# Row preparation of six experts from GpSimd to VectorE, in a planned attention and mixture-of-experts kernel

## The chip, the cores and the metric

The kernel runs on one core of a Trainium2 chip. Its engines are TensorE (PE: matmuls, with PEld for the loading of weights), VectorE (DVE), ScalarE (ACT), GpSimd (POOL) and SyncE (SP), each with a queue of its own that it works through in order, and 16 DMA engines that move data between HBM and the on-chip memories SBUF and PSUM. The metric is device microseconds of one execution; the median of several runs counts.

## The reference

```python
# attention without softmax: 8 batches x 8 heads, sequence 576, head size 64
kv  = einsum('bhsd,bhse->bhde', k, v)
out = einsum('bhsd,bhde->bhse', q, kv)
out = out / sqrt(mean(out*out, -1) + 1e-6) * g_norm
x   = out.transpose(0, 2, 1, 3).reshape(4608, 512)
# top-1 mixture of experts: 8 experts, D = 512, F = 1024, capacity 1152
logits = x @ w_gate; e = argmax(logits, 1); gate = softmax(logits)[e]
for each expert e:                      # its tokens in order, up to the capacity
    y = relu(x[tokens] @ w1[e]) @ w2[e]
    out[tokens] = gate * y              # tokens over the capacity: 0
```

All tensors are fp32.

## The kernel before

The first part of the execution (about its first quarter) computes attention and writes the un-normalized rows, with their norm factors and the gate, to `x_dram`: 4608 rows of 8 x (64 + 8) columns. Then the experts are worked through in order of their load, r = 0 to 7, with fixed budgets of 704, 672, 640, 624, 592, 576, 560 and 512 rows, so 6, 6, 5, 5, 5, 5, 5 and 4 tiles of up to 128 rows.

fp32 products are made from f16 halves: a value's high half is its f16 rounding, its low half the f16 rounding of the rest, and a product is high x high + high x low + low x high. Both the weights and the rows of an expert have to be split so.

For an expert beside the products of the one before (`rows_beside`), each tile of rows is gathered by POOL's indirect DMA (`xg`, L438), normalized (`xm` = `xg` x norm factor, `norm`, L446), its gate column copied (`gt`, L453, POOL), its high half cast by ScalarE (`pair_high`, L472), its low half made as `xm` - high (`pair_low`, L476), and the pair transposed into `xs` by a DMA of SP (L481). For the second expert (r = 1) the plan may put `xm` on VectorE or POOL, for the others on POOL alone; `pair_low` is always on POOL. Each POOL operation of the two is followed by an `engine_nop`.

The weights (`weights`, `split_weight`) come in fp32 to `raw` by eight DMAs of SP. VectorE takes the largest absolute value per partition (`am`, L342, eight per matrix; `a`, L350), multiplies that of w1 by the norm's weight `gcol`, one value per partition (L352); TensorE turns it to a row (`pt_max`, L355), VectorE takes the maximum (`bm`, L359), TensorE spreads it to all partitions (L362), VectorE makes a power of two of it (`bmax`, `ew`, `sw`, L366 and L300 to L309) and for w1 multiplies that by `gcol` (`sg`, L371). Then ScalarE makes the high halves `w1h`, `w2h` (L376) and VectorE the low ones `w1l`, `w2l` (L382), eight pieces each.

The products of an expert (`products`): for each of eight j, the first gemm makes a block `hp` in PSUM from 24 matmuls (two column halves each while there are over 512 rows: 16 with `w1h` and the high halves of the rows, then with their low halves; 8 with `w1l`; the trace merges them as x16 and x8). ScalarE makes `hh` = relu(`hp`) in f16 (L535), VectorE the rest `hl` (L538). `hp` has two banks: the product for j + 2 waits for `hl` of j. The second gemm makes `yp` (L576, narrow tiles L585, turned back by VectorE's copy `yt` L591 and TensorE L596), ScalarE scales it by the gate (`ysb`, L601), and POOL scatters it to the output (L606).

What stands in which order is set by one planner (`Plan`). Each operation has ways (engine and planned duration), what it depends on, a key, buffers that it takes from rings (`xg` 4, `xm` 2, `pair` 2, `xs` 2, `h` 2), and `late`, a time added to the earliest start that its dependencies allow. The planner places whatever can start first, the lower key ahead, and the program is issued on each engine in the planned order. At run time an engine holds to that order: an instruction that has to wait keeps all that stand behind it.

Of the kernel before, what the change touches and what calls it, by code (L numbers as in the profile page):

```python
# [15 lines left out]
ALU = mybir.AluOpType  # L16
# [29 lines left out]
FIRST = -50.0  # L46
# [21 lines left out]
NORM = 1.22  # L68
PAIR = 1.33
TURN = 1.25  # L70
TURNED = 1.3
GATHER = 1.2


class Hold:
# [91 lines left out]
def attention_moe_kernel(  # L167
# [12 lines left out]
    nc = tc.nc  # L180
# [4 lines left out]
    P = 128  # L185
# [143 lines left out]
    def split_weight(i, ws, raw, pieces=8):  # L329

        z = {}
# [16 lines left out]
        def most():  # L348
            z["a"] = a1 = sm.tile([P, 1], F32, name=f"a1_{i}")
            nc.vector.tensor_reduce(out=a1, in_=am(), axis=AX.X, op=ALU.max)  # L350
            if i == 0:
                nc.vector.tensor_tensor(out=a1, in0=a1, in1=gcol, op=ALU.mult)  # L352

        def across(pt):
            nc.tensor.transpose(pt[0:1, 0:P], z["a"], ident)  # L355
# [8 lines left out]
        def scale(pb):  # L364
            z["b"] = sm.tile([P, 1], F32, name="bmax")
            nc.vector.tensor_copy(z["b"], pb[:, 0:1])  # L366
            z["e"] = exponent(z["b"], 30, f"ew{i}")
            z["s"] = pow2(z["e"], -1, (256, 268)[i], f"sw{i}")
            if i == 0:
                sg = sm.tile([P, 1], F32, name="sg")  # L370
                nc.vector.tensor_tensor(out=sg, in0=z["s"], in1=gcol, op=ALU.mult)  # L371
                z["s"] = sg

        def high(p, e="A"):
# [45 lines left out]
    class Rows:  # L420
# [50 lines left out]
            self.pair[i] = self.pool.tile([P, 2, DM], F16, name="pair", bufs=2)  # L471
            nc.scalar.copy(self.pair[i][0:n, 0], self.xm[i][0:n])  # L472

        def pair_low(self, i):
            n, pair = self.part(i)[1], self.pair[i]
            nc.gpsimd.tensor_tensor(out=pair[0:n, 1], in0=self.xm[i][0:n], in1=pair[0:n, 0], op=ALU.subtract)  # L476
            nc.gpsimd.engine_nop()

        def pair_turn(self, i):
            x, n, _ = self.part(i)  # L480
# [187 lines left out]
    op = plan.op  # L668
# [857 lines left out]
    def weights(r, key, after, after2):  # L1526

        ws, sets, zs, holds = wsets[r % 2], [], [], []
        for i in range(2):
# [29 lines left out]
                f["across"](x.t[:, 128:256])  # L1559

            o = op(("V", 0.3), lambda e, f=f: f["most"](), tops, FIRST)
            o = op(("T", 0.12), across, [o], FIRST, (x,), late=2.0)
            o = op(("V", 0.2), lambda e, f=f, x=x: f["across_max"](x.t[:, 128:256]), [o], FIRST, (), (x,))
            o = op(("T", 0.06), lambda e, f=f, x=x: f["back"](x.t[:, 0:1]), [o], FIRST, (), (x,), late=1.0)
            ew = new(f"e{i}")
            o = op(("V", 1.1), lambda e, f=f, x=x: f["scale"](x.t[:, 0:1]), [o], FIRST, (ew,), (x,))
            zs.append((z, o, ew))
# [9 lines left out]
    def rows_beside(r, key):  # L1577
# [9 lines left out]
        for i in range(n):  # L1587
            xg, xm, pair = new("xg"), new("xm"), new("pair")

            def fetch(e, i=i):  # L1590
                if i == 0:
                    st["x"] = Rows(mo, st["gi"], 0, BUDGET[r], BM, 4)
                st["x"].fetch(i)

            o = op(("P", 1.05), fetch, [cut_, first] + early.get(("lows", r - 1), [])[-1:], key, (hold, xg), (sl,))
            first = first or o
            asked.append(o)
            o = op(("D", GATHER), None, [o], key, (), (xg,))
            a = op([("V", 0.61), ("P", NORM)] if r == 1 else ("P", NORM),
                   lambda e, i=i: st["x"].norm(i, nc.vector if e == "V" else nc.gpsimd), [o], key - 5 if r == 1 else key + 1,  # L1600
                   (xm,), (xg,))
            gates.append(op(("P", 0.25), lambda e, i=i: st["x"].gate(i, nc.gpsimd), [a], key + 1, (), (xg, hold)))
            a = op(("A", 0.52), lambda e, i=i: st["x"].pair_high(i), [a], key + 1, (pair,), (xm, hold))
            a = op(("P", PAIR), lambda e, i=i: st["x"].pair_low(i), [a], key + 1, (), (xm, pair, hold))
            if r == 1:
                early.setdefault(("lows", r), []).append(a)
            a = op(("S", TURN), lambda e, i=i: st["x"].pair_turn(i), [a], key + 1, (), (pair, hold))
            sent.append(a)
            turned.append(op(("D", TURNED), None, [a], key + 1, (), (pair, hold)))
# [107 lines left out]
```

## Time and profile before

| | us |
|---|---|
| median of three timed runs | 569.93 (567.73 to 570.16) |
| profiled execution | 566.6 |
| its span | 564.8 |
| TensorE busy | 520.2 (92%) |
| VectorE busy | 382.5 (68%) |
| ScalarE busy | 252.7 (45%) |
| GpSimd busy | 207.1 (37%) |

The busy share of an engine is an average over the attention part and the experts, which have other limits; it is read stretch by stretch below. A wait is put down to the operation whose end released it. The mean granted clock of TensorE in the profiled execution is 0.981 of full speed.

### The profile page before, as it was taken

How to read it: one execution, taken by the hardware profiler on the slowest of the kernel's cores; microseconds unless marked ns; L12 is line 12 of the kernel's file. 1: busy time of each engine (PE TensorE's matmuls, PEld its weight loads, DVE VectorE, ACT ScalarE, POOL GpSimd, SP SyncE). 2: the span in 40 equal slices, each digit the busy share in tenths (PEclk: the TensorE clock that was granted, in tenths of full speed). 3: DMA queues.
4: the chain of work that ended last, by engine and by line, in shares of the span. 5: the costliest groups of instructions: out<-in, count | busy, mean ns of one | idle time of the engine just before them, and what ended most of it. 6: DMA issues, size and time to landing. Idle time of an engine off the chain costs nothing.

```text
span 564.8 us, 12345 instructions
## 1 busy us (share of the span) xinstructions
PE 520.2 (92%) x4727; PEld 343.2 (61%) x4727; DVE 382.5 (68%) x978; ACT 252.7 (45%) x508; POOL 207.1 (37%) x233
## 2 busy tenths in 40 slices
PE   4989897978979997998999999999999999999995
PEld 4878786855536564544664575487467648745442
DVE  4468899899949979999997286367729606721200
ACT  1748684876313661644633526252544525202210
POOL 3011013552255684755225640644373171012011
PEclk9979996999999998999999999999999999999999
DMA  8999999592277687795938562664666151001001
GB/s 278 376 354 301 384 390 373 176 317 96 96 232 254 144 302 166 201 306 132 277 109 236 112 224 66 169 171 161 167 140 214 39 114 39 1 38 40 0 30 40
DMA packets 78020, 102.60 MB, mean 182 GB/s; under 512 B 43222, under 2 KB 51414, under 8 KB 76932
## 3 DMA queue, kind: packets, MB, share of 16 engines
q1 hardware_dynamic: 69600, 70.43, 42.5%
q0 software_dynamic: 7776, 31.30, 15.6%
q8 instruction: 39, 0.64, 0.5%
q14 instruction: 25, 0.20, 0.1%
q10 hardware_dynamic: 580, 0.02, 0.1%
HBM read 73.13 MB, written 20.61 MB: 166 GB/s over the span
## 4 chain that ended last, share of the span: by engine, by line
PE 26%; issue 16%; DMA 5%; DVE 3%; POOL 1%; ACT 1%; POOLq 0%; DVEq 0%; ACTq 0%
PE yp L576 12%; PE hp L530 12%; DMA out_dram<-ysb,si 5%; DVE w2l L382 1%; PE yp L585 1%; POOL xg L438 1%; DVE hl L538 1%; ACT w1h L376 0%; ACT w2h L376 0%; POOL xm L446 0%; POOLq L1652 0%; POOL pair L476 0%; POOL out_dram L606 0%; PE pt_max L355 0%; PE pt_max L362 0%
## 5 line engine op out<-in xcount | busy, mean ns | idle before, releaser
L530 PE MATMUL hp<-xs,w1h 128*128 128x320 f16 (+6 forms) x896 | 134.4, 301 | 5.1 <-DVE hl L538 4.5
L530 PEld LDWEIGHTS <-w1h 128*128 128x128 f16 x960 | 93.4, 98 | 47.1 <-issue 8.8
L576 PEld LDWEIGHTS <-hh 128*128 128x128 f16 x560 | 54.4, 98 | 65.5 <-issue 2.9
L606 POOL DMA_INDIRECT out_dram<-ysb,si x41 | 42.8, 1043 | 137.3 <-ACT ysb L601 99.6
L535 ACT ACTIVATE hh<-hp 128x320 f16<-128x320 f32 (+7 forms) x64 | 40.8, 638 | 114.5 <-PE hp L530 111.9
L342 DVE TENSOR_REDUCE am<-raw 128x1 f32<-128x512 f32 x120 | 75.6, 673 | 4.1 <-DMA raw<-in_moe_w_dram 3.8
L530 PE MATMUL hp<-xs,w1l 128*128 128x320 f16 (+6 forms) x448 | 72.0, 301 | 0.0
L538 DVE SCALAR_TENSOR_TENSOR hl<-hp,hh 128x320 f16<-128x320 f32 (+7 forms) x64 | 47.2, 737 | 32.9 <-ACT hh L535 32.8
L476 POOL TENSOR_TENSOR pair<-xm,pair 128x512 f16<-128x512 f32 (+5 forms) x35 | 44.7, 1278 | 66.5 <-ACT pair L472 61.8
L576 PE MATMUL yp<-w2h,hh 128*128 128x512 f16 x272 | 64.4, 379 | 0.8 <-ACT ysb L601 0.8
L576 PE MATMUL yp<-w2l,hh 128*128 128x512 f16 x272 | 64.6, 379 | 0.0
L576 PE MATMUL yp<-w2h,hl 128*128 128x512 f16 x272 | 64.3, 379 | 0.0
L601 ACT ACTIVATE ysb<-yp,ysc 128x512 f32<-128x512 f32 (+5 forms) x40 | 27.3, 684 | 82.4 <-PE yp L576 73.1
L382 DVE SCALAR_TENSOR_TENSOR w2l<-raw,sw,w2h 128x512 f16<-128x512 f32 x64 | 53.8, 885 | 10.7 <-ACT w2h L376 9.9
L530 PEld LDWEIGHTS <-w1l 128*128 128x128 f16 x480 | 46.9, 98 | 19.5
L438 POOL DMA_INDIRECT xg<-x_dram,gi x41 | 42.3, 1031 | 40.1 <-DVE gi L640 27.0
L382 DVE SCALAR_TENSOR_TENSOR w1l<-raw,sg,w1h 128x512 f16<-128x512 f32 x64 | 47.5, 797 | 0.9 <-ACT w1h L376 0.8
L576 PEld LDWEIGHTS <-hl 128*128 128x128 f16 x280 | 27.0, 98 | 31.9
L823 PE MATMUL op<-kv_bd,qt 128*128 128x144 f32 x256 | 42.6, 310 | 3.7 <-ACT qt L676 1.3
L376 ACT ACTIVATE w2h<-raw,sw 128x512 f16<-128x512 f32 x62 | 39.8, 711 | 5.2 <-DVE p2t L307 2.1
L376 ACT ACTIVATE w1h<-raw,sg 128x512 f16<-128x512 f32 x60 | 38.3, 711 | 7.2 <-DVE sg L371 7.1
L823 PEld LDWEIGHTS op<-kv_bd,qt 128*128 128x128 f32 x256 | 36.7, 206 | 6.0 <-ACT qt L676 2.2
(246 smaller groups left out, 688.7 us busy)
## 6 DMA issues: line engine op xcount, KB each, us to landing
raw<-in_moe_w_dram SPq DMA_DIRECT2D x64, 512.0 KB
k_sb<-in_k_dram SPq DMA_DIRECT2D x16, 576.0 KB
v_sb<-in_v_dram SPq DMA_DIRECT2D x16, 576.0 KB
x_dram<-o_sb POOLq DMA_DIRECT2D x8, 1152.0 KB
q_sb<-in_q_dram SPq DMA_DIRECT2D x16, 512.0 KB
x_dram<-o_sb POOLq DMA_DIRECT2D x8, 144.0 KB
q_sb<-in_q_dram SPq DMA_DIRECT2D x32, 32.0 KB
xg<-x_dram,gi POOLq DMA_INDIRECT x41
```

Source lines behind the costliest of these rows:

```text
L342: nc.vector.tensor_reduce(out=am()[:, p:p + 1], in_=raw[:, sl(p)], axis=AX.X, op=ALU.max, apply_absolute_value=True)
L376: nc.scalar.activation(wh[:, sl(p)], raw[:, sl(p)], AF.Copy, scale=z["s"])
L382: nc.vector.scalar_tensor_tensor(out=wl[:, sl(p)], in0=raw[:, sl(p)], scalar=z["s"], in1=wh[:, sl(p)], op0=ALU.mult, op1=ALU.subtract)
L438: nc.gpsimd.indirect_dma_start(out=self.xg[i][0:n], out_offset=None, in_=x_dram[0:self.rows, :], in_offset=bass.IndirectOffsetOnAxis(ap=se ...
L476: nc.gpsimd.tensor_tensor(out=pair[0:n, 1], in0=self.xm[i][0:n], in1=pair[0:n, 0], op=ALU.subtract)
L530: nc.tensor.matmul(self.view(hp)[:, u], lhsT=w[:, c, j * P:(j + 1) * P], rhs=x[:, c, u * hw:(u + 1) * hw], start=(t == 0 and c == 0), stop ...
L535: nc.scalar.activation(self.out(self.hh, j), self.view(hp), AF.Relu)
L538: nc.vector.scalar_tensor_tensor(out=self.out(self.hl, j), in0=self.view(hp), scalar=0.0, in1=self.out(self.hh, j), op0=ALU.max, op1=ALU.s ...
L576: nc.tensor.matmul(yp[0:n, 0:DM], lhsT=h[:, j, o:o + n], rhs=w[:, j, :], start=(m == 0), stop=(m == len(self.terms) - 1))
L601: nc.scalar.activation(self.ysb[0:n], yp[0:n, 0:DM], AF.Copy, scale=self.ysc[0:n, i:i + 1])
L606: nc.gpsimd.indirect_dma_start(out=out[:, :], out_offset=bass.IndirectOffsetOnAxis(ap=self.sidx[0:n, col:col + 1], axis=0), in_=ysb[0:n], ...
L823: nc.tensor.matmul(y, lhsT=qt.t[:, i * P:(i + 1) * P], rhs=kv2[:, half * HH + i], start=True, stop=True)
```

## The change

From the third expert on (r = 2 to 7), `norm` and `pair_low` are operations of VectorE (planned 0.64 us each) and no longer of POOL (1.22 and 1.33); `norm` is planned at least 3.0 us (`LANDED`) later than before after its gather. The gate's copy stays on POOL, and so do both operations for r = 1. The two products with `gcol` become `tensor_scalar` with `gcol` as the scalar operand. In the plan, `across` (the transpose of the maximum) is late by 5.0 in place of 2.0, `back` by 3.0 in place of 1.0. Lines behind L72 move down by 1, those behind `pair_low` by 2.

```diff
--- before.py
+++ after.py
@@ -70,6 +70,7 @@
 TURN = 1.25
 TURNED = 1.3
 GATHER = 1.2
+LANDED = 3.0
 
 
 class Hold:
@@ -349,7 +350,7 @@
             z["a"] = a1 = sm.tile([P, 1], F32, name=f"a1_{i}")
             nc.vector.tensor_reduce(out=a1, in_=am(), axis=AX.X, op=ALU.max)
             if i == 0:
-                nc.vector.tensor_tensor(out=a1, in0=a1, in1=gcol, op=ALU.mult)
+                nc.vector.tensor_scalar(out=a1, in0=a1, scalar1=gcol, scalar2=None, op0=ALU.mult)
 
         def across(pt):
             nc.tensor.transpose(pt[0:1, 0:P], z["a"], ident)
@@ -368,7 +369,7 @@
             z["s"] = pow2(z["e"], -1, (256, 268)[i], f"sw{i}")
             if i == 0:
                 sg = sm.tile([P, 1], F32, name="sg")
-                nc.vector.tensor_tensor(out=sg, in0=z["s"], in1=gcol, op=ALU.mult)
+                nc.vector.tensor_scalar(out=sg, in0=z["s"], scalar1=gcol, scalar2=None, op0=ALU.mult)
                 z["s"] = sg
 
         def high(p, e="A"):
@@ -471,10 +472,11 @@
             self.pair[i] = self.pool.tile([P, 2, DM], F16, name="pair", bufs=2)
             nc.scalar.copy(self.pair[i][0:n, 0], self.xm[i][0:n])
 
-        def pair_low(self, i):
+        def pair_low(self, i, eng=nc.gpsimd):
             n, pair = self.part(i)[1], self.pair[i]
-            nc.gpsimd.tensor_tensor(out=pair[0:n, 1], in0=self.xm[i][0:n], in1=pair[0:n, 0], op=ALU.subtract)
-            nc.gpsimd.engine_nop()
+            eng.tensor_tensor(out=pair[0:n, 1], in0=self.xm[i][0:n], in1=pair[0:n, 0], op=ALU.subtract)
+            if eng is nc.gpsimd:
+                nc.gpsimd.engine_nop()
 
         def pair_turn(self, i):
             x, n, _ = self.part(i)
@@ -1559,9 +1561,9 @@
                 f["across"](x.t[:, 128:256])
 
             o = op(("V", 0.3), lambda e, f=f: f["most"](), tops, FIRST)
-            o = op(("T", 0.12), across, [o], FIRST, (x,), late=2.0)
+            o = op(("T", 0.12), across, [o], FIRST, (x,), late=5.0)
             o = op(("V", 0.2), lambda e, f=f, x=x: f["across_max"](x.t[:, 128:256]), [o], FIRST, (), (x,))
-            o = op(("T", 0.06), lambda e, f=f, x=x: f["back"](x.t[:, 0:1]), [o], FIRST, (), (x,), late=1.0)
+            o = op(("T", 0.06), lambda e, f=f, x=x: f["back"](x.t[:, 0:1]), [o], FIRST, (), (x,), late=3.0)
             ew = new(f"e{i}")
             o = op(("V", 1.1), lambda e, f=f, x=x: f["scale"](x.t[:, 0:1]), [o], FIRST, (ew,), (x,))
             zs.append((z, o, ew))
@@ -1596,12 +1598,14 @@
             first = first or o
             asked.append(o)
             o = op(("D", GATHER), None, [o], key, (), (xg,))
-            a = op([("V", 0.61), ("P", NORM)] if r == 1 else ("P", NORM),
-                   lambda e, i=i: st["x"].norm(i, nc.vector if e == "V" else nc.gpsimd), [o], key - 5 if r == 1 else key + 1,
-                   (xm,), (xg,))
+            by_letter = {"V": nc.vector, "P": nc.gpsimd}
+            a = op([("V", 0.61), ("P", NORM)] if r == 1 else ("V", 0.64),
+                   lambda e, i=i: st["x"].norm(i, by_letter[e]), [o], key - 5 if r == 1 else key + 1,
+                   (xm,), (xg,), late=0.0 if r == 1 else LANDED)
             gates.append(op(("P", 0.25), lambda e, i=i: st["x"].gate(i, nc.gpsimd), [a], key + 1, (), (xg, hold)))
             a = op(("A", 0.52), lambda e, i=i: st["x"].pair_high(i), [a], key + 1, (pair,), (xm, hold))
-            a = op(("P", PAIR), lambda e, i=i: st["x"].pair_low(i), [a], key + 1, (), (xm, pair, hold))
+            a = op(("P", PAIR) if r == 1 else ("V", 0.64), lambda e, i=i: st["x"].pair_low(i, by_letter[e]), [a], key + 1, (),
+                   (xm, pair, hold))
             if r == 1:
                 early.setdefault(("lows", r), []).append(a)
             a = op(("S", TURN), lambda e, i=i: st["x"].pair_turn(i), [a], key + 1, (), (pair, hold))
```

Two places show how the order moves. First VectorE in the second expert's first gemm, where `hl` is this expert's and `am`, `a` are maxima of the third expert's weights. Before:

```order
L382 SCALAR_TENSOR_TENSOR w2l_2715<-raw_2711,sw_3342,w2h_2714 128x512 x2
L538 SCALAR_TENSOR_TENSOR hl<-hp,hh 128x672
L382 SCALAR_TENSOR_TENSOR w2l_2715<-raw_2711,sw_3342,w2h_2714 128x512 x2
L342 TENSOR_REDUCE am_3492<-raw_151 128x1
L538 SCALAR_TENSOR_TENSOR hl<-hp,hh 128x672
L342 TENSOR_REDUCE am_3492<-raw_151 128x1 x5
L538 SCALAR_TENSOR_TENSOR hl<-hp,hh 128x672
L342 TENSOR_REDUCE am_3492<-raw_151 128x1 x2
L342 TENSOR_REDUCE am_3555<-raw_2711 128x1
L350 TENSOR_REDUCE a_0_3567<-am_3492 128x1
L352 TENSOR_TENSOR a_0_3567<-a_0_3567,gcol 128x1
```

Two `w2l`, then maxima, stand between one `hl` and the next here. With the change, from the second of these `hl` on; `xm` and `pair` are the third expert's rows:

```order
L540 SCALAR_TENSOR_TENSOR hl<-hp,hh 128x672
L383 SCALAR_TENSOR_TENSOR w2l_2715<-raw_2711,sw_3365,w2h_2714 128x512 x3
L540 SCALAR_TENSOR_TENSOR hl<-hp,hh 128x672
L383 SCALAR_TENSOR_TENSOR w2l_2715<-raw_2711,sw_3365,w2h_2714 128x512 x2
L447 TENSOR_TENSOR xm<-xg 128x512 x2
L540 SCALAR_TENSOR_TENSOR hl<-hp,hh 128x672
L477 TENSOR_TENSOR pair<-xm,pair 128x512 x2
L343 TENSOR_REDUCE am_3347<-raw_151 128x1 x2
L540 SCALAR_TENSOR_TENSOR hl<-hp,hh 128x672
L343 TENSOR_REDUCE am_3347<-raw_151 128x1
L447 TENSOR_TENSOR xm<-xg 128x512 x2
L343 TENSOR_REDUCE am_3347<-raw_151 128x1
```

The `w2l` of the second expert stand ahead of what they stood behind, and between two `hl` there are now up to five operations, `xm` and `pair` among them.

POOL at the same place, before: `xg` are gathers of the third expert's rows, ISA is the `engine_nop`.

```order
L438 DMA xg<-x_dram,gi_2817 128x576
L446 TENSOR_TENSOR xm<-xg 128x512
L449 ISA
L476 TENSOR_TENSOR pair<-xm,pair 128x512
L477 ISA
L453 COPY gt<-xg 128x1
L476 TENSOR_TENSOR pair<-xm,pair 128x512
L477 ISA
L446 TENSOR_TENSOR xm<-xg 128x512
```

Tile by tile, gathers alternate here with `xm`, `pair` and `gt`. With the change:

```order
L439 DMA xg<-x_dram,gi_2817 128x576
L454 COPY gt<-xg 128x1
L439 DMA xg<-x_dram,gi_2817 128x576
L454 COPY gt<-xg 128x1 x4
L439 DMA xg<-x_dram,gi_2849 128x576 x4
L608 DMA out_dram<-ysb,si_2789 4608x512
L454 COPY gt<-xg 128x1
```

Gathers and gate copies follow one another, and those of the fourth expert (another `gi`) come right behind.

## Rows read from the trace of the kernel before

**Rows 1.** Part 1 of the page: busy us, share of the span, instructions

```profile
PE 520.2 (92%) x4727; PEld 343.2 (61%) x4727; DVE 382.5 (68%) x978; ACT 252.7 (45%) x508; POOL 207.1 (37%) x233
```

**Rows 2.** Stretches; columns: us, then per engine busy (instructions), PEclk, DMA share, GB/s

```profile
200.00:260.00 60.00, 54.22 (x309) 30.42 (x310) 56.42 (x98) 28.30 (x46) 37.29 (x41) 0.97 0.79 238
260.00:300.00 40.00, 38.55 (x339) 25.86 (x337) 38.21 (x78) 22.86 (x37) 13.19 (x15) 1.00 0.63 183
300.00:500.00 200.00, 199.55 (x1494) 128.33 (x1493) 118.68 (x280) 78.58 (x127) 79.90 (x90) 1.00 0.48 128
```

**Rows 3.** What TensorE waited for, 195 to 565: us in total, times, longest

```profile
PE hp L530 <- DVE hl L538: 4.5, 3, 3.7
PE pt_max L362 <- DVE bm L359: 2.2, 2, 1.2
PE yp L596 <- DVE yt L591: 0.7, 1, 0.7
PE hp L530 <- DMA xs<-pair: 0.5, 1, 0.5
PE pt_max L355 <- DVE a L352: 0.5, 1, 0.5
```

**Rows 4.** Timeline of TensorE: start us, us, engine, line, operation [idle before <-releaser]

```profile
207.14 2.44 PE L530 MATMUL hp<-xs,w1h 128*128 128x336 f16 x16
...
210.56 2.44 PE L530 MATMUL hp<-xs,w1h 128*128 128x336 f16 x16
...
217.85 3.73 PE L530 MATMUL hp<-xs,w1h 128*128 128x336 f16 x16 [3.70 <-DVE hl L538]
...
222.94 2.44 PE L530 MATMUL hp<-xs,w1h 128*128 128x336 f16 x16
...
265.74 2.34 PE L530 MATMUL hp<-xs,w1h 128*128 128x320 f16 x16
```

**Rows 5.** Timeline of VectorE, same columns

```profile
209.04 0.86 DVE L538 SCALAR_TENSOR_TENSOR hl<-hp,hh 128x672 f16<-128x672 f32 x1 [0.25 <-ACT hh L535]
209.82 6.62 DVE L382 SCALAR_TENSOR_TENSOR w2l<-raw,sw,w2h 128x512 f16<-128x512 f32 x2
...
216.96 0.84 DVE L538 SCALAR_TENSOR_TENSOR hl<-hp,hh 128x672 f16<-128x672 f32 x1
...
240.21 6.60 DVE L382 SCALAR_TENSOR_TENSOR w2l<-raw,sw,w2h 128x512 f16<-128x512 f32 x8
...
252.26 2.88 DVE L352 TENSOR_TENSOR a<-a,gcol 128x1 f32<-128x1 f32 x1
...
260.53 2.66 DVE L371 TENSOR_TENSOR sg<-sw,gcol 128x1 f32<-128x1 f32 x1
```

**Rows 6.** Lines L382 and L446 on VectorE: ns min/median/max, first and last start, forms

```profile
L382 DVE SCALAR_TENSOR_TENSOR w2l<-raw,sw,w2h x64: 715/741/5954, 141.3 to 477.7; 128x512 f16<-128x512 f32 x64
...
L446 DVE TENSOR_TENSOR xm<-xg x7: 681/693/1735, 161.6 to 193.1; 128x512 f32<-128x512 f32 x5, 64x512 f32<-64x512 f32 x1, 32x512 f32<-32x512 f32 x1
```

**Rows 7.** Timeline of GpSimd

```profile
209.69 1.07 POOL L446 TENSOR_TENSOR xm<-xg 128x512 f32<-128x512 f32 x1
...
215.19 1.28 POOL L453 COPY gt<-xg 128x1 f32<-128x1 f32 x2
...
250.74 2.30 POOL L476 TENSOR_TENSOR pair<-xm,pair 128x512 f16<-128x512 f32 x2
253.02 2.09 POOL L446 TENSOR_TENSOR xm<-xg 128x512 f32<-128x512 f32 x2
...
259.83 2.29 POOL L476 TENSOR_TENSOR pair<-xm,pair 128x512 f16<-128x512 f32 x2
```

**Rows 8.** Part 5 of the page: busy us, mean ns of one, idle before, releaser

```profile
L342 DVE TENSOR_REDUCE am<-raw 128x1 f32<-128x512 f32 x120 | 75.6, 673 | 4.1 <-DMA raw<-in_moe_w_dram 3.8
```

**Rows 9.** The waits of all engines

```profile
POOL pair L476 <- ACT pair L472: 61.8, 10, 13.3
```

**Rows 10.** Timeline of VectorE, earlier

```profile
167.94 0.68 DVE L446 TENSOR_TENSOR xm<-xg 64x512 f32<-64x512 f32 x1 [2.21 <-DMA xg<-x_dram,gi]
```

## The prediction

> **What bounds the kernel now.** I read the busy shares first, then a table of stretches, then what TensorE waited for, then the timelines of the three engines around the longest wait. TensorE is busy for 520.2 of 564.8 us [rows 1], and from 300 to 500 for 199.55 of 200 [rows 2]: whatever is saved ahead of that stretch moves its dense work up and shortens the span by as much, and nothing can be gained inside it. What is left lies in 200 to 300, where 5.8 and 1.45 us of TensorE are idle [rows 2]. The waits from 195 on sum to 8.4 us [rows 3]: 4.5 for `hl`, 2.2 for `bm`, 0.5 for `a` (all three made by VectorE, DVE), 0.7 for `yt` and 0.5 for a transpose's DMA.
>
> The longest of them is the key. In the second expert's first gemm a group of products starts every 3.42 us (207.14, 210.56); the next one is due at 213.98, but starts at 217.85 after 3.70 us without work [rows 4]. It waits for `hl` at 216.96, and that stood on DVE behind two `w2l` that began at 209.82 and took 6.62 us [rows 5], where two cost 1.48 at the median of 741 ns and one took 5954 ns [rows 6]. In that time GpSimd (POOL) worked on `xm`, `pair` and `gt` from 209.69 to 216.47 [rows 7], and `w2l` ended when POOL did. After the wait TensorE is slow for one group: 5.09 us to the start of the next (222.94), not 3.42 [rows 4], 1.67 us more. [...]
>
> The same pattern stands twice more: `a` x `gcol` (one element per partition) takes 2.88 us at 252.26, beside POOL's `pair` and `xm` from 250.74 to 255.11, and `sg` = `sw` x `gcol` takes 2.66 us at 260.53, beside a `pair` run that begins at 259.83 [rows 5, 7]. So in this trace a DVE instruction with two operands in SBUF stands still while POOL runs back to back on tiles in SBUF, to the end of POOL's run and not of one instruction.
>
> [...]
>
> **The change part by part.** The third to eighth expert have 5, 5, 5, 5, 5 and 4 tiles of rows, 29 in all; for each, one `xm` and one `pair` leave POOL for DVE.
>
> 1. The hold in the second expert's gemm. The POOL run beside it belongs to the third expert's rows, so it goes; in the new order POOL has there only gathers and one-column copies. `w2l` then costs its median, `hl` comes on time, and the 3.70 us and the 1.67 us behind it go: 5.37 us. Late next in that group would be `hl` behind the new `xm` and `pair`, which step 5 counts.
>
> 2. The two tiny products. Their waits on TensorE are 0.5 for `a` and 2.2 for `bm` (two of them, one behind each of the held products) [rows 3]: 2.7 us. They go twice over: POOL's run is gone, and the product reads `gcol` as a scalar, not as a second tensor. Between nothing and 2.7 I take 2.7.
>
> 3. The other two waits for `hl`, 4.5 - 3.7 = 0.8 us [rows 3], also stand behind `w1l` and `w2l` of a slot that the new order fills otherwise. 0 to 0.8; I take 0.8, as long POOL runs are gone there too.
>
> 4. Margins. The transposes of the maxima (`pt_max`) are planned 3 and 2 us later after what they need. Their real waits are under 1.2 us [rows 3], so TensorE meets them ready. What comes later is the scale and with it `w1h`, `w1l`, `w2h`, `w2l` of the next expert. For the third expert that has room: its first gemm starts at 265.74 [rows 4], some 9 us earlier after the gain, and its `w2l` is done at 246.81 [rows 5], 10 us ahead of that. The second expert has none: its `w2l` is still being made inside its own first gemm, at 209.82 [rows 5]. There 0.7 for `yt` and 0.5 for the DMA can go [rows 3], or up to 5 us of planned lateness appear. I take +0.5, with -3 to +1.2 as the ends.
>
> 5. What it costs on DVE. 58 instructions at the nearest row, `xm` on DVE, of which seven are there with 681, 693 and 1735 ns [rows 6]: 40 us at the median, 39 to 101 at the ends. `pair` on DVE is not in the trace; it has the same shape and also two SBUF operands, so it gets the same row. I take 40. That lies beside TensorE: DVE is busy 118.68 of 200 us from 300 to 500 [rows 2], and 10 instructions per expert are 7 us in some 50. From 200 to 300 it is busy 94.63 of 100, but that includes the holds, 5.2 us of it in the one `w2l` (5.954 - 0.741). With the 5.4 that DVE is idle there, 10.6 us of room against 7 of new work an expert.
>
> What counts there is `hl`. One that came on time ran from 209.04 to 209.90, 0.66 us before the group that needs its bank (210.56) [rows 4, 5], and took 0.86. Per 3.42 us DVE has 3.42 - 0.86 = 2.56 for other work. By the new order the work between `hl`s is two `w2l` and two `xm` (2.9 us), two `pair` and two `am` (2.7), then two `am`, two `xm` and a `pair` (3.4), with `am` at 673 ns [rows 8]. Over 2.56 each that is 0.3, 0.2 and 0.9, summed 1.4 us late, against 0.66 that is free: about 0.7 us of wait. Ends: 0, and a stall of 5.4 each time (the second rival). I take -0.7.
>
> 6. What POOL loses, 29 `xm` and 29 `pair`, shortens nothing: it is busy 37% [rows 1]. Gathers and scatters may start earlier. The gathers wait for free `xg` slots, which DVE now frees; the ring has four. 0.
>
> The sum is 5.37 + 2.7 + 0.8 + 0.5 - 0.7 = 8.7 us. The profiled run took 566.6 us, 1.8 of it outside its span; it would take 557.9. It is 3.3 us below the median of the three timed runs, 569.93 (567.73 to 570.16). As the terms are waits of the order and not of one run, I take them off the median: **561.2 us**.
>
> **The rivals.**
>
> A smaller gain. The wider margins push the second expert's scales back, and its first product waits for `w1h` or `w1l` at about 200. Up to 5 us are planned, some of it is covered by the 1.2 us that TensorE waits there already: about 3 us less, 569.9 - 6 = 564. For it: the second expert's scales have no time in hand (step 4). Against: the second expert's last `pair`, which is what TensorE waits for last, comes earlier in the new order.
>
> Slower: DVE takes over POOL's waits. POOL's `pair` waited for ScalarE's cast 61.8 us in 10 places, up to 13.3 [rows 9], and a DVE `xm` waited 2.21 us for its gather [rows 10]. POOL can stand there at no cost. On DVE everything behind it stands too, `hl` first, and `hl` has 0.66 us. A wait like that hold costs what the hold costs, 3.70 + 1.67 = 5.4 us. One such stall in three of the six experts, 16.2, against 8.7 is +7.5: 577. It decides from a second stall on (8.7 / 5.4 = 1.6). For it: the 61.8. Against: ScalarE's cast waited on POOL's `xm` itself, DVE's is faster, and the order puts other DVE work between an `xm` and its `pair` (`hl` or `am`), and leaves 3 us after a landing.
>
> The hold is not POOL's. If 5.954 us for one `w2l` came from elsewhere, the stalls stay, and DVE has 10 more instructions, 6.9 us, in a stretch that is full: 569.9 + 6.9, again about 577. [...] Against: two holds end where POOL's runs end (216.44 and 216.47, 255.14 and 255.11), and the third begins inside one [rows 5, 7].
>
> No gain. The stalls go but the next work waits for something as late: the third expert's rows or weights, needed 9 us earlier: 569.9. For it: no row gives the landing of the third expert's transposes in the new order. Against: the weights have 10 us in hand (step 4), and DMA is at 0.79 of its time in this stretch only, 0.63 and 0.48 behind it [rows 2].
>
> **How the numbers follow.** The forecast (558 to 563.5): 0.50. Smaller gain: 0.22. No gain: 0.10. DVE's waits: 0.11. Another cause of the hold: 0.03. More gain, to below 556: 0.04. A measurement of this kernel, with timed runs 0.43% apart, can tell about 0.5% from no change, 2.8 us. Faster: 0.50 + 0.22 + 0.04 = 0.76; the same: 0.10; slower: 0.14. From 556 to 571 only the last case and the two slow ones are left out, 0.18.
>
> **What would show it.** Right: no DVE `w2l` above 2 us from 200 on, groups of the second expert's first gemm 3.42 us apart throughout, `bm` and `a` gone from TensorE's waits, the third expert's products starting at about 257, DVE up by some 30 us in its busy time (40 less the holds). Wrong: `hp` waiting for `hl` again with DVE's own wait for ScalarE's `pair` or a gather ahead of it; TensorE waiting for `w1h` or `w1l` near 200; or `w2l` held though POOL only moves rows.

## The result and the profile after

| | us |
|---|---|
| median with the change, 20 runs | 563.57 (559.96 to 568.55) |
| median before, 20 runs | 569.71 (565.47 to 574.35) |
| ratio, 95% interval | 0.9892 [0.9869, 0.9915] |
| profiled execution, span | 562.91, 561.1 |

The change makes the kernel 6.1 us faster (1 - 0.9892 of 569.71; 4.8 to 7.5 by the interval). 561.2 was forecast, 8.7 us below the first median of 569.93: the direction holds, the time lies within the range, and the gain is 2.6 us short.

Busy time of the profile after (part 1 of the page). VectorE is up 20 us on [rows 1], not the 30 that were forecast; GpSimd loses 58.

```profile
PE 518.4 (92%) x4727; PEld 342.6 (61%) x4727; DVE 402.6 (72%) x1037; ACT 253.3 (45%) x508; POOL 148.8 (27%) x174
```

The three stretches (us, busy time and instructions of PE, PEld, DVE, ACT, POOL, PEclk, DMA share, GB/s), against [rows 2]: TensorE now has 1.46 and 0.56 us idle in the first two, not 5.8 and 1.45, and 0.96 from 300 to 500, where it had 0.45. The granted clock is 1.00 in the first, where it was 0.97. Before, it was 0.50 of full speed from 218.9 to 222.2, in the slow group of products behind the long wait; half of these 3.3 us is 1.7 us, about the 1.67 that this group took more. That is gone too.

```profile
200.00:260.00 60.00, 58.54 (x466) 34.89 (x463) 52.38 (x103) 29.52 (x48) 23.91 (x25) 1.00 0.83 239
260.00:300.00 40.00, 39.44 (x285) 25.12 (x281) 33.29 (x72) 19.74 (x31) 9.87 (x11) 1.00 0.62 169
300.00:500.00 200.00, 199.04 (x1494) 127.89 (x1492) 150.92 (x346) 83.50 (x133) 42.69 (x53) 1.00 0.51 134
```

What TensorE waited for from 195 on (us in total, times, longest), against [rows 3]: `bm`, `a` and the DMA are gone, `yt` doubled, and `hl` still costs 1.1 us in two other places.

```profile
PE yp L598 <- DVE yt L593: 1.5, 1, 1.5
PE hp L532 <- DVE hl L540: 1.1, 2, 0.6
PE hp L532 <- DVE p2t L308: 0.3, 1, 0.3
```

TensorE's timeline at the second expert, against [rows 4]: behind the wait for `yt` the second group follows after 3.63 us (a product with `bm` lies between), the others every 3.42 us, and the third expert starts at 260.63, 56.5 us after the second, where it was 66.1 (199.60 to 265.74).

```profile
203.68 0.60 PE L598 MATMUL yp<-ident,yt 128*64 128x128 f32 x4 [1.46 <-DVE yt L593]
204.11 2.44 PE L532 MATMUL hp<-xs,w1h 128*128 128x336 f16 x16
...
207.74 2.44 PE L532 MATMUL hp<-xs,w1h 128*128 128x336 f16 x16
...
211.16 2.44 PE L532 MATMUL hp<-xs,w1h 128*128 128x336 f16 x16
...
214.58 2.44 PE L532 MATMUL hp<-xs,w1h 128*128 128x336 f16 x16
...
260.63 1.65 PE L532 MATMUL hp<-xs,w1h 128*128 128x320 f16 x11
```

VectorE's two lines of the low halves (ns min/median/max), against [rows 6]: no `w2l` is held any more (751 ns at most); one `w1l` still takes 2202.

```profile
L383 DVE SCALAR_TENSOR_TENSOR w1l<-raw,sg,w1h x64: 729/735/2202, 108.1 to 450.4; 128x512 f16<-128x512 f32 x64
L383 DVE SCALAR_TENSOR_TENSOR w2l<-raw,sw,w2h x64: 706/743/751, 145.4 to 473.8; 128x512 f16<-128x512 f32 x64
```

That one is in the eight `w1l` of the second expert, whose rows are still GpSimd's; `yt` stands behind them, and TensorE for `yt`:

```profile
195.26 7.74 DVE L383 SCALAR_TENSOR_TENSOR w1l<-raw,sg,w1h 128x512 f16<-128x512 f32 x8
...
203.13 0.40 DVE L593 COPY yt<-yp 128x256 f32<-128x256 f32 x1
```

The wait for `p2t` and the longer one for `hl` (0.32 and 0.64 us) begin in the fourth expert's gemm: VectorE stands 5.25 us on the copy of an index table (`si`), which waits for a scatter that still reads the buffer, and `hl` stands behind.

```profile
319.85 0.17 DVE L642 COPY si<-sidx_tab 128x6 int32 x1 [5.25 <-DMA out_dram<-ysb,si]
...
320.99 0.80 DVE L540 SCALAR_TENSOR_TENSOR hl<-hp,hh 128x624 f16<-128x624 f32 x1
```

The shorter wait for `hl`, 0.49 us in the third expert's gemm (at 271.73), has another cause. VectorE waited 1.90 us for ScalarE's cast, and from then on the work ahead of that `hl` is late:

```profile
264.80 0.69 DVE L477 TENSOR_TENSOR pair<-xm,pair 128x512 f16<-128x512 f32 x1 [1.90 <-ACT pair L473]
```

VectorE's own waits of these two kinds, 200 to 500. ScalarE's cast is what the slower rival named; here it is 10.3 us in 11 places:

```profile
DVE pair L477 <- ACT pair L473: 10.3, 11, 3.6
...
DVE si L642 <- DMA out_dram<-ysb,si: 5.7, 2, 5.2
```

### The profile page after: what moved, and what is told of

Read it like the earlier page. It is cut to its first block, busy times and chain, and to the rows that moved or that the text cites. A ratio compares the mean times of both kernels' runs of the same rounds, so it can differ in the third digit from the quotient of the medians.

```text
span 561.1 us, 12271 instructions
## 1 busy us (share of the span) xinstructions
PE 518.4 (92%) x4727; PEld 342.6 (61%) x4727; DVE 402.6 (72%) x1037; ACT 253.3 (45%) x508; POOL 148.8 (27%) x174
## 4 chain that ended last, share of the span: by engine, by line
PE 44%; issue 18%; DVE 17%; DMA 16%; ACT 2%; POOL 1%; POOLq 0%; SPq 0%; DVEq 0%; ACTq 0%
PE hp L532 18%; PE yp L578 13%; DMA out_dram<-ysb,si 10%; PE op L825 4%; DVE w1l L383 3%; DMA q_sb<-in_q_dram 2%; DVE ss L858 2%; PE qp L807 2%; PE a L736 1%; PE yp L587 1%; DVE am L343 1%; DVE hl L540 1%; DMA xg<-x_dram,gi 1%; DMA v_sb<-in_v_dram 1%; DMA xs<-pair 1%
## 5 line engine op out<-in xcount | busy, mean ns | idle before, releaser
L608 POOL DMA_INDIRECT out_dram<-ysb,si x41 | 47.2, 1150 | 243.9 <-ACT ysb L603 197.6
L439 POOL DMA_INDIRECT xg<-x_dram,gi x41 | 40.5, 988 | 43.0 <-DVE xm L447 10.4
L383 DVE SCALAR_TENSOR_TENSOR w2l<-raw,sw,w2h 128x512 f16<-128x512 f32 x64 | 44.3, 741 | 0.4 <-ACT w2h L377 0.4
L473 ACT CAST pair<-xm 128x512 f16<-128x512 f32 (+5 forms) x35 | 21.3, 613 | 28.1 <-DMA xs<-pair 20.1
```

What stands on the lines that cost most here:

```text
L383: nc.vector.scalar_tensor_tensor(out=wl[:, sl(p)], in0=raw[:, sl(p)], scalar=z["s"], in1=wh[:, sl(p)], op0=ALU.mult, op1=ALU.subtract)
L439: nc.gpsimd.indirect_dma_start(out=self.xg[i][0:n], out_offset=None, in_=x_dram[0:self.rows, :], in_offset=bass.IndirectOffsetOnAxis(ap=se ...
L608: nc.gpsimd.indirect_dma_start(out=out[:, :], out_offset=bass.IndirectOffsetOnAxis(ap=self.sidx[0:n, col:col + 1], axis=0), in_=ysb[0:n], ...
```

## The experiments

All ratios are to the kernel before, runs on the same chip, 95% interval in brackets. The kernels ran on several chips, on which the kernel before has medians of 568.5 to 570.6, so kernels of different chips are best compared by their ratios. Beside the time I use a second measure: the part of the span from the first expert's first product to the end. The order ahead of that product is the same in all kernels, yet it starts between 131.2 and 135.4 us in eleven profiles, so a span of one profile carries about 4 us that no edit explains. These are the first product before, and after:

```profile
131.18 1.60 PE L530 MATMUL op<-xs,w1h 128*128 128x384 f16 x8 [0.31 <-DVE xs L678]
```

```profile
135.28 1.60 PE L532 MATMUL op<-xs,w1h 128*128 128x384 f16 x8 [0.31 <-DVE xs L680]
```

The part of the experts is thus 564.8 - 131.2 = 433.6 before and 561.1 - 135.3 = 425.8 after, 7.8 us less, though the spans differ by 3.7 only. This measure is not free of chance either. The move alone and the change with the old margins have the same order on every engine, and their parts are 424.4 and 427.1; 1.9 us of that arise before the second expert starts, where with the old margins eight `yp` products take 2.54 us at 171.45 and eight `hp` 2.33 at 173.79 (1.89 and 1.25 a few us later). A difference of less than about 3 us in the last column shows nothing by itself.

| kernel | median us | ratio | experts' part, us |
|---|---|---|---|
| before | 569.7 | 1 | 433.6 |
| the change | 563.57 | 0.9892 [0.9869, 0.9915] | 425.8 |
| move alone | 560.28 | 0.9841 [0.9802, 0.988] | 424.4 |
| scalar operands alone | 568.08 | 0.9968 [0.9939, 0.9996] | 432.3 |
| margins alone | 568.25 | 0.9976 [0.9941, 1.001] | 431.8 |
| change, move of the third expert alone | 566.38 | 0.9947 [0.9917, 0.9976] | 429.6 |
| change, move from the fourth on | 567.98 | 0.9974 [0.9941, 1.0006] | 431.7 |
| change, old margins | 560.2 | 0.9835 [0.9787, 0.9883] | 427.1 |
| the same, second expert moved too | 562.41 | 0.9864 [0.9818, 0.9911] | 429.4 |
| old margins, no wait for landing | 565.53 | 0.9941 [0.9907, 0.9975] | 431.0 |
| change, no margins | 567.92 | 0.9999 [0.9964, 1.0033] | 431.2 |

**The move alone**, against the change:

```diff
-            o = op(("T", 0.12), across, [o], FIRST, (x,), late=5.0)
+            o = op(("T", 0.12), across, [o], FIRST, (x,), late=2.0)
...
-                nc.vector.tensor_scalar(out=a1, in0=a1, scalar1=gcol, scalar2=None, op0=ALU.mult)
+                nc.vector.tensor_tensor(out=a1, in0=a1, in1=gcol, op=ALU.mult)
...
```

> Only the move of norm and pair_low to VectorE (with its 3 us after a landing); gcol products as two-tensor products and the plan's margins as before. Theory 1 (a DVE instruction with two SBUF operands stands still while GpSimd works through a run of tensor instructions): no w2l above 2 us from 200 us on, no 3.7 us wait of TensorE for hl, and 5 to 8 us faster than before, at least as much as the whole change (6.1), since nothing pushes the second expert's scales back. Theory 2 (it is the wider margins that reorder DVE so that hl stands ahead of w2l): 0 to 2 us faster, the wait for hl still there.

Measured: 9.1 us faster (6.8 to 11.3), and TensorE's waits from 195 on (same columns as above) hold no `hl`, `a` or `bm`:

```profile
PE yp L598 <- DVE yt L593: 0.7, 1, 0.7
PE yp L578 <- ACT hh L537: 0.6, 1, 0.6
PE hp L532 <- DMA xs<-pair: 0.5, 1, 0.5
```

Theory 2 falls: the move gives all of the gain and more, without the margins. Theory 1 fits; but the move also gives VectorE another order, so what a run on GpSimd does to VectorE is shown only by the programs at the end of this section.

**The scalar operands alone**, on the kernel before:

```diff
-                nc.vector.tensor_tensor(out=a1, in0=a1, in1=gcol, op=ALU.mult)
+                nc.vector.tensor_scalar(out=a1, in0=a1, scalar1=gcol, scalar2=None, op0=ALU.mult)
...
```

> Only the two gcol products as tensor_scalar; the order on every engine is that of before. Theory 1: w2l is held as before and the wait of 3.7 us for hl stays; if an instruction with gcol as scalar operand is not held, the waits for a and bm (2.7 us) go and the time falls by 2 to 3 us; if it is held all the same, the time is that of before within 1 us. Theory 2: no change.

Measured: 1.8 us faster (0.2 to 3.5). `a` takes 0.21 us in all eight places:

```profile
L352 DVE TENSOR_SCALAR a<-a,gcol x8: 212/214/215, 95.0 to 413.6; 128x1 f32<-128x1 f32 x8
```

VectorE's timeline, and GpSimd's beside it. The product at 257.20 passes in 0.21 us beside a GpSimd run, where it stood for 2.88 before; `w2l` at 214.22 is held as before, and the run that used to hold `sg` now holds `w1l`:

```profile
214.22 6.94 DVE L382 SCALAR_TENSOR_TENSOR w2l<-raw,sw,w2h 128x512 f16<-128x512 f32 x2
...
257.20 0.21 DVE L352 TENSOR_SCALAR a<-a,gcol 128x1 f32<-128x1 f32 x1
...
265.33 5.32 DVE L382 SCALAR_TENSOR_TENSOR w1l<-raw,sg,w1h 128x512 f16<-128x512 f32 x3
```

```profile
256.10 2.29 POOL L476 TENSOR_TENSOR pair<-xm,pair 128x512 f16<-128x512 f32 x2
258.38 2.09 POOL L446 TENSOR_TENSOR xm<-xg 128x512 f32<-128x512 f32 x2
```

So the products with the scalar operand were not held (`a` 0.21 us in all eight places, `sg` too), but beside GpSimd's run at 265.44 `w1l`, with two tensors, was held: 5.32 us for three, where the median of one is 0.742. TensorE's waits for `a` and `bm` are gone, and 1.2 us for `p2t` have come behind the held `w1l`: some of the 2.7 us came, not all.

**The margins alone**, on the kernel before:

```diff
-            o = op(("T", 0.12), across, [o], FIRST, (x,), late=2.0)
+            o = op(("T", 0.12), across, [o], FIRST, (x,), late=5.0)
...
-            o = op(("T", 0.06), lambda e, f=f, x=x: f["back"](x.t[:, 0:1]), [o], FIRST, (), (x,), late=1.0)
+            o = op(("T", 0.06), lambda e, f=f, x=x: f["back"](x.t[:, 0:1]), [o], FIRST, (), (x,), late=3.0)
```

> Only the wider margins (5.0 and 3.0 for 2.0 and 1.0); xm and pair stay on GpSimd. Theory 1: some w2l of the second expert is still held for several us beside GpSimd's run on the third expert's rows, TensorE waits 3 us or more for hl in that gemm, and the time is that of before or up to 3 us longer, as the second expert's scales also come later. Theory 2: the stall is gone and the time falls by 4 to 6 us.

Measured: 1.4 us faster, not clear of none. TensorE waits as long as before in sum, in other places:

```profile
PE hp L530 <- DVE p2t L307: 2.5, 1, 2.5
PE yp L596 <- DVE yt L591: 2.5, 2, 1.4
PE hp L530 <- DVE hl L538: 2.1, 2, 1.5
```

Theory 1 said 3 us or more for `hl` in the second expert's gemm; it was 1.5. The new order moved GpSimd's run against `w2l`, and the longest `w2l` in that gemm is 1.64 us (2.98 in the whole run). What a margin does through the order is not to be read from its size.

**The move for the third expert alone, and for the fourth to eighth alone**, each with the rest of the change (`norm` and `pair_low` on VectorE under the condition shown, else on GpSimd as before):

```diff
-            a = op([("V", 0.61), ("P", NORM)] if r == 1 else ("V", 0.64),
+            a = op([("V", 0.61), ("P", NORM)] if r == 1 else (("V", 0.64) if r == 2 else ("P", NORM)),
...
-            a = op(("P", PAIR) if r == 1 else ("V", 0.64), lambda e, i=i: st["x"].pair_low(i, by_letter[e]), [a], key + 1, (),
+            a = op(("V", 0.64) if r == 2 else ("P", PAIR), lambda e, i=i: st["x"].pair_low(i, by_letter[e]), [a], key + 1, (),
```

> The whole change, but xm and pair only of the third expert on VectorE (10 instructions in place of 58); those of the fourth to eighth stay on GpSimd. Theory 1: the long hold was beside the third expert's rows alone, so 5 to 7 us of gain remain, and DVE has 33 us less to do. Theory 2: as with the margins alone. A third view (the gain comes from a lighter GpSimd in all experts): about a sixth of 6.1, 1 us.

> The whole change, but the third expert's xm and pair stay on GpSimd; the fourth to eighth expert's are on VectorE. Theory 1 (GpSimd's runs hold VectorE): w2l in the second expert's first gemm is held beside the third expert's rows as with the margins alone (a wait of 1.5 us or more for hl at about 220), and no w1l or w2l is held behind 245 us, so about 2 to 4 us faster than before: the other part of what the third expert alone gave (3.2 us). If the third expert's rows were all that matters: within 1 us of the margins alone.

Measured: 3.0 us faster, and 1.5 (not clear of none); with the margins' 1.4 taken off, 1.6 and 0.1. It was expected that the third expert's rows carry nearly all; they do not, and the two parts do not add up to the whole (each leaves GpSimd runs, and in the first the longest `w1l` takes 4.37 us and the longest `w2l` 4.16, in the second 2.20 and 1.64). With the third expert alone the long wait for `hl` is gone, but TensorE waits 2.0 us for `hh` and 1.5 for `yt`. With the others alone TensorE waits 1.1 us for `hl` at 219.53, behind two `w2l` of 1.64 us beside the third expert's rows, as expected; but its longest wait for `hl` is 3.1 us at 276, and the cause is no hold: VectorE stands on `si` behind a scatter.

```profile
275.13 0.17 DVE L642 COPY si<-sidx_tab 128x6 int32 x1 [3.73 <-DMA out_dram<-ysb,si]
...
275.28 0.81 DVE L540 SCALAR_TENSOR_TENSOR hl<-hp,hh 128x640 f16<-128x640 f32 x1
```

**The change with the margins of before**, the move alone plus scalar operands (the same order as the move alone):

> The change with the margins of before (2.0 and 1.0): move and scalar operands. If the wider margins cost what the trace of the move alone shows (1.5 us at yt near 204, and waits of 0.3 to 0.6 for hl and p2t at 267 to 326), it is as fast as the move alone, about 560 to 561 us, and 2 to 3 us faster than the whole change. If the scalar operands matter once GpSimd has no runs, faster than the move alone by over 1 us; I expect no difference, as gcol's products took 0.16 us there against 0.21 with the scalar. If the margins cost nothing, 563.6.

Measured: 560.2, as the move alone (560.28). So the scalar operands do nothing that can be told once these runs have left GpSimd, and the wider margins cost about 3 us (ratio 0.9892 against 0.9835 here and 0.9841 for the move alone; the intervals just overlap). The profiles do not show where: the experts' part of the change is 1.4 us longer than that of the move alone and 1.3 shorter than that of this kernel, which is within what one order differs by. These two are the fastest versions found, 1.6% under before; the change is at 1.1%.

**The second expert moved too**, on that one (both lines without the case for `r == 1`):

> Margins of before, scalar operands, and the second expert's xm and pair on VectorE as well (it has 6 tiles, so up to 12 instructions more). If GpSimd's runs on these also hold w1l at about 195 to 203 (8 w1l took 7.74 us with the change, 5.94 at the median), 0 to 1.5 us faster than the move alone: 559 to 560. If VectorE is what ends last between 160 and 200 us (28.8 of 30 us busy from 170 to 200 before), 2 to 5 us slower than that.

Measured: 562.4, 2.2 us slower than without it, not clear of none (the intervals overlap). No `w1l` takes over 1.26 us any more, where 1.64 was the longest with these rows on GpSimd, so the hold near 200 was GpSimd's. But TensorE now waits 1.4 us for `a`, 0.8 for `bm` and 1.5 for `hl`: in the second expert's gemm VectorE stands twice for ScalarE's cast (2.42 and 2.44 us, at 228.14 and 232.06), with `hl` and `a` behind.

**No wait for the landing**, on the change with old margins:

```diff
-LANDED = 3.0
+LANDED = 0.0
```

> The change with the margins of before and without the 3 us after a landing (LANDED = 0): the same work on the same engines, but xm is planned on VectorE right behind the planned landing. If VectorE standing for gathers is a price of this move (the slower rival): VectorE waits 2 to 4 us for xg several times, TensorE waits for hl again, and it is 3 to 10 us slower than the change with the margins of before (560.2). If VectorE's waits are hidden by the slack of hl: within 1 us of 560.2.

Measured: 5.3 us slower than with it (6.0 by the ratios). VectorE's timeline shows it standing for ScalarE's cast and for a gather:

```profile
235.25 0.69 DVE L477 TENSOR_TENSOR pair<-xm,pair 128x512 f16<-128x512 f32 x1 [4.70 <-ACT pair L473]
...
261.03 0.69 DVE L447 TENSOR_TENSOR xm<-xg 112x512 f32<-112x512 f32 x1 [2.52 <-DMA xg<-x_dram,gi]
```

TensorE waits 1.7 us for `hh`, which stands on ScalarE behind that same cast, then 1.3 for `a`, which stands on VectorE behind one more wait for a cast (1.47 us), then 0.8 and 0.5. In sum VectorE waits hardly longer for casts than with the 3 us (12.2 us against 10.7, 200 to 500); what differs is which of these waits stand ahead of TensorE's work. The slower rival's mechanism is real, and the 3 us of the change keep it off the path.

**No margin on the transposes** (`late=0.0` twice, in the change):

> The change with no margin at all on the two transposes (0 and 0 in place of 5.0 and 3.0; 2.0 and 1.0 gave 560.2, 5.0 and 3.0 563.6). If a margin only delays the scales, 0 to 1 us faster than 560.2, with the waits for yt and the DMA near 204 unchanged. If it keeps TensorE from meeting an unready transpose, TensorE waits for a and bm (0.3 to 1 us each, up to 14 of each in the experts) and it is 1 to 5 us slower than 560.2.

Measured: 567.9, the whole gain gone. The place is near 200: from the first expert's remaining rows to the second expert 33.0 us pass, 28.7 with the change. TensorE pauses six times there, 3.2 us in all, with nothing that the profile names, and its granted clock falls to 0.69 from 205 to 210. Neither expectation fits: TensorE's waits for `a` are 0.5 us in all. What the pauses are stays open, and with them most of this loss.

**The hold by itself.** Three programs without the kernel's work: ScalarE releases a run of GpSimd instructions and one to six VectorE ones. The GpSimd runs of the second and third are made of this kernel's operations (X = `xm`, R = `pair`, G = `gt`); `w_low` is an instruction like `w1l` or `w2l`.

```python
def pool_run(n, kind="two", nop=False, same=False):   # the first program
    for k in range(n):
        src, pout = g if k == 0 else a, pouts[0 if same else k]
        if kind == "two":
            nc.gpsimd.tensor_tensor(out=pout, in0=src, in1=b, op=ALU.mult)
...
for n in range(80):                                   # added in the third
    nc.sync.dma_start(raws[n % 4], ...)
...
test(1, "XRGRXXGG")
test(2, "XFXRGRXXGG")     # F: an indirect DMA of 128 rows
```

> The hold by itself: no attention and no experts, the output is zeros. ScalarE releases a run of 0 to 6 GpSimd instructions (128x512, two operands, one operand, or 128x1 copies) and a VectorE maximum of 0.67 us with one VectorE instruction behind it. If a VectorE instruction with two operands in SBUF stands still to the end of GpSimd's run: w_low takes 0.74 us beside nothing and about 0.1 + k x 1.05 beside k instructions: 1.1, 2.2, 4.3, 6.4 us for k = 1, 2, 4, 6. If it waits for one instruction at most: 0.74 to 1.9 us whatever k is. With gcol as a scalar operand (one value per partition) about 0.2 us beside a run, as a second tensor some 3.5 us; the low half from PSUM 0.6 to 0.8 us, not held. Six w_low in a row beside four: the first held, the others not.

VectorE's rows, in order: beside nothing, beside one, beside six GpSimd products, beside six one-operand ones, then the one-column product as a tensor and with a scalar operand beside four:

```profile
8.64 0.74 DVE L48 SCALAR_TENSOR_TENSOR low<-a,col,wh 128x512 f16<-128x512 f32 x1
...
13.18 1.31 DVE L48 SCALAR_TENSOR_TENSOR low<-a,col,wh 128x512 f16<-128x512 f32 x1
...
39.49 1.31 DVE L48 SCALAR_TENSOR_TENSOR low<-a,col,wh 128x512 f16<-128x512 f32 x1
...
59.13 0.74 DVE L48 SCALAR_TENSOR_TENSOR low<-a,col,wh 128x512 f16<-128x512 f32 x1
...
73.66 0.72 DVE L54 TENSOR_TENSOR one<-mid,col 128x1 f32<-128x1 f32 x1
...
80.12 0.20 DVE L57 TENSOR_SCALAR one<-mid,col 128x1 f32<-128x1 f32 x1
```

My reading of the trace before, that a hold lasts to the end of GpSimd's run, fails here: it is 1.31 us beside one product and beside six, and GpSimd stands for VectorE in turn (1.71 in place of 1.22 us). The low half with one operand in PSUM took 0.68 us beside four products.

> As the hold alone, but GpSimd's run is made of this kernel's own operations: X = xm (128x512, one operand a column repeated over 64), R = pair (f16 out, f32 and f16 in), G = gt (128x1 copy), T = the plain f32 product of the first study, with and without an engine_nop behind each; VectorE's w_low arrives 0.15 us (or 0.67) after the run begins. In the first study w_low stood for one instruction only, whatever the run's length (1.31 us), and GpSimd then stood for VectorE. In the kernel one stood for six (5.954 us). If a kind of operation (X or R) lets GpSimd go on without giving way: w_low takes 3.5 us or more beside XXXX or RRRR, and 5 to 6 us in XRGRXXGG. If early arrival does it: 4 us or more beside TTTT too. If neither, all are 1.3 to 1.9 us, and the kernel's long hold needs something else, such as other engines or DMAs at work.

Measured: 0.74 to 1.84 us in all 32. Neither these kinds of operations nor the nops nor an early arrival gave a longer hold.

> What made the kernel's hold last over six GpSimd instructions (5.954 us), where the two studies of it alone gave one instruction (1.3 to 1.8 us)? The same runs of X, R and G with their engine_nop, each with two w_low, now first with loads of 512 KB going on from the start of the program, and again without them; with a gather (F) of 128 rows in the run; with eight ScalarE operations of 0.6 us beside it; and with an operation from PSUM on VectorE just ahead. If DMA traffic does it, w_low takes 4 us or more in the first half and 1.3 to 1.8 in the second; if the gather does it, only with F, in both halves; if ScalarE or the PSUM operation, only there. If all stay under 2 us, the length of the kernel's hold stays open. The output is zeros.

Two `w_low` each: without and with a gather in the run, with loads going on (first two rows) and without (last two):

```profile
21.95 3.06 DVE L98 SCALAR_TENSOR_TENSOR low<-a,col,wh 128x512 f16<-128x512 f32 x2
...
36.42 6.27 DVE L98 SCALAR_TENSOR_TENSOR low<-a,col,wh 128x512 f16<-128x512 f32 x2
...
129.34 2.99 DVE L98 SCALAR_TENSOR_TENSOR low<-a,col,wh 128x512 f16<-128x512 f32 x2
...
143.74 6.09 DVE L98 SCALAR_TENSOR_TENSOR low<-a,col,wh 128x512 f16<-128x512 f32 x2
```

GpSimd beside the last of them: the gather, then `xm`, `pair`, `gt`, `pair`, two `xm`, none of them slowed (in the run without a gather the first `pair` and the `gt`, at 130.21 and 131.75, took 1.57 and 0.62 us).

```profile
141.97 1.02 POOL L65 DMA_INDIRECT xf<-in_q_dram,idx  x1 [0.17 <-issue]
143.01 1.05 POOL L72 TENSOR_TENSOR xm<-xg 128x512 f32<-128x512 f32 x1
144.03 1.16 POOL L75 TENSOR_TENSOR pair<-b,wh 128x512 f16<-128x512 f32 x1
145.15 0.18 POOL L77 COPY gt<-xg 128x1 f32<-128x1 f32 x1
145.30 1.14 POOL L75 TENSOR_TENSOR pair<-b,wh 128x512 f16<-128x512 f32 x1
146.43 2.05 POOL L72 TENSOR_TENSOR xm<-xg 128x512 f32<-128x512 f32 x2
```

With the gather two `w_low` took 6.27 and 6.09 us, without it 3.06 and 2.99; the longest single one took 5479 ns (5954 in the kernel). The loads changed it by 0.2 us at most. In all six runs behind a gather the first `w_low` stood until the last `xm` had ended (3.88 to 5.48 us); without a gather 1.54 us was the most. The two differ in one more thing, four maxima on VectorE ahead of `w_low`, so that it arrives behind the gather; a later arrival without a gather gave 1.52 us at most in the second program. The three long holds of the kernel before began so too, with a gather or a scatter right ahead of GpSimd's runs at 209.69, 250.74 and 259.83:

```profile
207.74 1.94 POOL L438 DMA_INDIRECT xg<-x_dram,gi  x1 [0.27 <-POOL gt L453]
...
249.68 1.04 POOL L606 DMA_INDIRECT out_dram<-ysb,si  x1 [5.47 <-DMA raw<-in_moe_w_dram]
...
258.82 0.98 POOL L606 DMA_INDIRECT out_dram<-ysb,si  x1 [2.21 <-DMA out_dram<-ysb,si]
```

In that trace all six VectorE instructions with two SBUF tensors that took over 1.9 us stand beside such a run; beside runs without a DMA right ahead none took over 1.64 us. With the margins alone GpSimd stood 0.39 us between a gather and its run at 212.03, and no `w2l` beside that took over 1.64 us either. Why the longest holds came behind a DMA is not shown, and a scatter was not run by itself.

## Why the prediction was right, and short by 2.6 us

1. The hold in the second expert's gemm, 5.37: right. The move alone takes it away, and the groups are 3.42 us apart.

2. The two products, 2.7: right in size. From the second expert's third group to the third expert's first product 49.5 us pass (260.63 - 211.16), 58.6 before (265.74 - 207.14 [rows 4]): 9.1 us less, where steps 1 and 2 came to 8.1. Part of the rest is two pairs of transposes that now come later. "They go twice over" holds for the two waits, which the scalar operand alone takes away as well, but not for the time: alone it leaves a hold to `w1l` (5.32 us for three) and gives 1.8 us, and on top of the move it adds nothing.

3. The other waits for `hl`, +0.8, and step 5's cost of -0.7: +0.1 forecast. 1.45 us of waits (0.49, 0.32 and 0.64) stand where 0.8 stood: -0.65. In the second expert's gemm, where step 5 put its 0.7, the work between `hl`s costs TensorE nothing. The waits lie behind it: 0.49 us in the third expert's gemm, behind VectorE's 1.90 us for a cast, which is the slower rival's mechanism in small, and 0.96 in the fourth's, behind VectorE on `si`, waiting 5.25 us for a scatter. I had counted VectorE's waits for casts and gathers, and not the copies that wait for GpSimd's scatters.

4. Margins, +0.5: the step that failed. `yt` rose from 0.7 to 1.46 as `w1l` now ends just ahead of it, held beside the second expert's `pair` on GpSimd (2.20 us for one, at 197.91); the DMA's 0.5 went. From the first expert's first product to the second expert's third group the trace has 75.88 us, 75.96 before: +0.1, not +0.5. In the timed runs the margins cost about 3 us, the far end of the range that I had given this step (-3), though the intervals of the kernels with and without them just overlap; where that time goes is open beyond `yt`. The waits on `si` do not follow the margins alone: 5.7 and 9.9 us with the change and with the move from the fourth on, none with the old margins, but 2.7 with the old margins and the second expert moved too, and none with the wide ones and the third expert alone. The rival "a smaller gain" named `w1l` at about 200, and that is the one that was held, with `yt` and TensorE behind it. Its 564 is nearer to the measured 563.57 than my 561.2.

5. The move's cost on VectorE, 40 us of new work beside TensorE: TensorE bears it. But VectorE's busy time rose by 20 only, not by the 30 forecast: the 58 at their median of 0.684 us are 39.7, so more held time went than I had counted.

6. The rivals. The slower one needed the landing's 3 us to be missing: without them 5.3 us are lost. "The hold is not GpSimd's" is refuted by the move alone and by the programs of the hold. Where I argued from the trace that a hold lasts to the end of the run, the argument was right for these runs (5.95 us for one `w2l`), but not for GpSimd's runs in general (1.31 us beside six products), and that an indirect DMA stood right ahead of each of the three was not in it.

The trace has 7.8 us less in the experts' part: +0.1 up to the second expert's third group, +9.1 from there to the third expert's first product (8.1 forecast), -1.4 behind it (300.5 us, 299.1 before). Steps 1 and 2 gave a microsecond more than reckoned, and steps 3 to 5, forecast at +0.6, gave -1.3; that these errors partly cancel in the sum is luck. The third expert's products, forecast at about 257, start at 260.63; 4.1 us of that lie ahead of the first expert's first product. The timed runs have 6.1 us (4.8 to 7.5); the difference is within what single profiles differ by.

## What to carry to other kernels

When one engine's instruction is many times its median (here 5.95 us against 0.741), look at what the neighbouring engine ran, and at what it had issued just before. Moving the small work to the engine that was being held can pay although that engine is fuller (here 9.1 us by the move alone, from an engine 37% busy to one 68% busy), if its waits (casts, landings, buffers that a scatter still reads) are planned and not met in front of the work that the critical engine needs (without the 3 us for a landing 5.3 us were lost). Bundle edits only after each has run alone: here, by the timed runs, about 3 of the move's 9 us went to two margins that alone showed no clear cost or gain.

## What the hardware showed that was not expected

- In the first program `w_low`, with two SBUF tensors, took 0.74 us beside nothing and 1.31 beside one and beside six GpSimd products. In the third, behind a gather, the first `w_low` took 3.88 to 5.48 us, until the last `xm` of GpSimd's run had ended; in the kernel before, one `w2l` took 5.95 us beside a run behind a gather.
- Beside six of GpSimd's one-operand `tensor_scalar` (128x512) `w_low` took 0.74 us, as beside nothing. Beside four GpSimd products a VectorE `tensor_scalar` of one value per partition took 0.20 us, the same product of two tensors 0.72 (0.16 at the median in the kernel before).
- The attention part with an unchanged order ended between 131.2 and 135.4 us in eleven profiles.
